# Outputs split by the parity of the position, all FFN-side stores on GpSimd's queue, x loaded for two tiles at once

## The chip, the cores and the metric

The kernel runs on one core of one Trainium2 chip. The metric is the device time of one execution in microseconds, the median over several runs. The engines are named as in the profile: PE (matrix multiply), DVE (vector), ACT (scalar), POOL (GpSimd) and SP (SyncE, which here only issues DMAs). SPq and ACTq are the instruction streams of SP and ACT in which DMA issues stand.

## What is computed

Two blocks follow one another. The first is a long convolution by FFT, per channel, over 4 batches of 12,544 positions with 128 channels; the second is a feed-forward network whose hidden layer is the largest of three products. Cut to what matters:

```
h_filt = (relu(pos_emb @ w1) @ w2) * exp(-0.01 * pos)[:, None]
u = x * v
y = irfft(rfft(u, n=2*S) * rfft(h_filt, n=2*S))[:, :S]      # along the positions
t = (x * y).reshape(B * S, 128)
h = max(t @ W1, t @ W2, t @ W3)                              # 768 hidden columns
out = h @ W_out                                              # 128 columns
```

## The kernel before

Everything is fp32. The 12,544 positions of a batch are 128 residues times 98 (NB). The host lays x and v out by channel, so that the 98 positions of one residue and one channel are one run of 392 bytes; the output is laid out the same way.

**Stages.** First come the filter's spectrum and the convolution of batch 0, with nothing beside them. Then follows the FFN, batch after batch, and beside the FFN of batch b stands the convolution of batch b+1; beside the FFN of batch 3 stands nothing.

**The FFN.** A tile is 4 residues, so 392 columns; a pair is two tiles, and a batch has 16 pairs. `t_load` (L521) brings a tile's part of the convolution's last stage, zt, and its x, xT, both on SP's queue. `t_last` (L538) does the last stage on PE into `yps` and multiplies with xT on DVE (L558, L560) into the tile `gt`, which has 4 buffers. `up` (L565) makes one block of 128 hidden rows: the product `pa`, ACT's Relu of it into `hid` (L570), the product `pb`, DVE's maximum (L573). `products` (L608) multiplies with W_out by a seven-product scheme of Strassen and Winograd's kind, over a 2 x 2 split: the hidden blocks in two halves and the two tiles of the pair; POOL forms its sums s1 to s4 (L589), PE its products into two PSUM banks (`mm`, L619), ACT and DVE the four results c11, c21, c12, c22 (`copied`, L628; `added`, L632). In these names the first index is the tile of the pair and the second the half of the 128 output columns. PE writes each half-tile (two residues) to its own 64 of the 128 partitions. `stored` (L634) writes each result with two DMAs of 49 KB on ACT's queue, so there are eight in a pair.

**The order of the work** is written out by hand. A pair has 12 steps, one for each call of `up`; a list `stream` holds what is due after each step (products 9 steps and more after the pair's start, `LAG`), `SUMS` (L605) the steps of POOL's sums, and `conv_steps` (L475) lays the next batch's convolution over the 192 steps of the batch. Each engine runs its instructions in that order. Within a step `up` comes first, then `stream`, then `t_last`, then the convolution's part. `t_load` is called in steps 0 and 1 of the pair before, `t_last` in steps 5 and 8.

**The convolution beside the FFN** has two phases. In the u phase, for each of 32 (26 for batch 1) units u: `u_load` loads x and v (L337, SP), `u_mul` multiplies (L344, DVE), `u_planes` splits the result into 16-bit planes (L364, L365, POOL), `u_dma` transposes them by DMA (L371, SP), `u_join` puts them together (L380, one half on ACT, one on DVE), `u_first` is the first FFT stage (L140, PE). With s the step of `u_join`, the others stand at s - 13, s - 7, s - 6 and s - 5. In the g phase, for each of 45 groups g: `w_load` and `h_load` (L396, L403, SP), `g_second` on PE, `g_butterfly` on DVE, `g_swap` on ACT, `g_re` and `g_im` on DVE (L430, L433), `g_sum` on POOL (L436), `g_unfold` on DVE (L442, into `ab`), `g_third` on PE (reads `ab` and a second `wt`), `g_pair` on DVE (L468) and `g_store` (L471, a 256 KB DMA on ACT's queue into `zd`). A new group begins about every 2.6 steps.

**Buffers and semaphores.** x and v of the u phase and both `wt` of the g phase share two buffers for each of two tags: the pool `inq` is made twice, and the second, with `bufs=2` (L857), is the one used. The list of instructions shows further that each DMA issued by SP or ACT signals one of eight semaphores (DMAHW0 to 7), taken in turn by both queues together, and that a DMA often waits for the semaphore of the eighth before it; DMAs issued by POOL have eight of their own (DMASW0 to 7).

```
            def stored(n, m, name):                       # L634
                for c in range(2):
                    p0 = 4 * (i + n) + 2 * c
                    nc.scalar.dma_start(dst[64 * m:64 * m + 64, p0:p0 + 2, b, :], ...)
    def t_load(b, i):                                     # L521
        xT = hp.tile([D, 4, NB], FP32, tag="xT", name="xT", bufs=2)
        for c in range(GC):
            nc.sync.dma_start(xT[c * NG:(c + 1) * NG], x[:, 4 * i:4 * i + 4, c, b, :])
```

Of the kernel before, what the change touches and what calls it, by code (L numbers as in the profile page):

```python
# [70 lines left out]
def kernel(  # L71
# [374 lines left out]
    def g_third(b, g):  # L446
        w, ab = ws.pop((g, 1)), abs_.pop(g)
        ps = state["cv"][1].tile([P, 512], FP32, tag="cv", name="ps3")
        for k in range(2):
            for q in range(2):  # L450
                halves_mm(ps[:, (2 * k + q) * D:(2 * k + q + 1) * D], w[:, k, q, :],
                          ab[:, k, q, :], k == 0 and q == 0, True)
        if b == 0:
            zs = state["cv"][0].tile([P, 2, 256], FP32, tag="z", name="zs", bufs=2)
            nc.scalar.copy(zs[:].rearrange("p k f -> p (k f)"), ps[:])
            zss[g] = zs
            g_store(b, g)
        else:
            z1 = state["cv"][0].tile([P, 256], FP32, tag="z1", name="z1", bufs=2)
            nc.scalar.copy(z1[:], ps[:, 256:512])  # L460
            zss[g] = ps, z1

# [58 lines left out]
    def t_load(b, i):  # L521
        zt = hp.tile([N1, 2, 512], FP32, tag="zt", name="zt", bufs=2)
        if b == 0:
            nc.sync.dma_start(
                zt[:], zd[b][:, :, 2 * i:2 * i + 2, :].rearrange("k c t f -> k c (t f)"))
        else:
            for c in range(2):
                nc.sync.dma_start(
                    zt[NK * c:NK * c + NK],
                    zd[b].rearrange("(g a) c t f -> g a c t f", a=2)[  # L530
                        :, :, c, 2 * i:2 * i + 2, :].rearrange("g a t f -> g a (t f)"))
        zts[b, i] = zt
        xT = hp.tile([D, 4, NB], FP32, tag="xT", name="xT", bufs=2)
        for c in range(GC):
            nc.sync.dma_start(xT[c * NG:(c + 1) * NG], x[:, 4 * i:4 * i + 4, c, b, :])
        xTs[b, i] = xT

    def t_last(i):  # L538
        zt = zts.pop(i)
        ps = cps.tile([P, 512], FP32, tag="cv", name="yps")  # L540
        g = hp.tile([D, 4, NB], FP32, tag="g", name="gt", bufs=4)
        y = ps[:, 0:N].rearrange("d (p n) -> d p n", p=4)
        if i[0] == 0:
            for s in range(4):
                for c in range(2):
                    halves_mm(y[:, s, :], zt[:, c, s * D:(s + 1) * D], f4[:, c, :],
                              s == 0 and c == 0, c == 1)
        else:

            h = NB // 2  # L550
            for s in range(4):
                for a in range(2):
                    halves_mm(y[:, s, a * h:a * h + h], zt[:, a, s * D:(s + 1) * D],
                              f4p[:, a, :], s == 0 and a == 0, True)
            y = y.rearrange("d p (a m) -> d p m a", a=2)
        xT = xTs.pop(i)
        if i[0] == 0:
            nc.vector.tensor_tensor(out=g[:], in0=y, in1=xT[:], op=ALU.mult)  # L558
        else:
            nc.vector.tensor_tensor(out=g[:].rearrange("d p (m a) -> d p m a", a=2), in0=y,  # L560
                                    in1=xT[:].rearrange("d p (m a) -> d p m a", a=2),
                                    op=ALU.mult)
        gs[i] = g

    def up(i, f, tag, bufs):  # L565
# [42 lines left out]
    def products(b, i, h, X, Y):  # L608
# [14 lines left out]
        def flat(g):  # L623
            return g[:].rearrange("d p n -> d (p n)")

        def copied(name, ps):
            t[name] = new(name) if name == "p1" else new("o", 3)
            nc.scalar.copy(t[name][:], ps[:, 0:H2])  # L628

        def added(name, a, ps):  # L630
            t[name] = new(name) if name in ("u2", "u3") else new("o", 3)
            nc.vector.tensor_tensor(out=t[name][:], in0=t[a][:], in1=ps[:, 0:H2], op=ALU.add)  # L632
# [9 lines left out]
        plan = (  # L642
            (X, "h11", wo_sb[:, 0:NC, 0:64], True, None, [(copied, "p1", X)], None),
            (Y, "s2", tw[:, 0], True, None, [(added, "u2", "p1", Y)], None),
            (X, "h12", wo_sb[:, NC:, 0:64], False, (m1, first), [(copied, "c11", X)],
             (stored, 0, 0, "c11")),
            (Y, "s3", tw[:, 1], False, (m2, second_), [(added, "u3", "p1", Y)], None),
            (X, "h21", wo_sb[:, 0:NC, 64:128], True, None, [(added, "c22", "u3", X)],
             (stored, 1, 1, "c22")),
            (Y, "h22", tw[:, 2], True, (linx[:], second_), [(added, "c21", "u3", Y)],  # L650
             (stored, 1, 0, "c21")),
            (X, "h12", wo_sb[:, NC:, 64:128], False, (m2, first), [(added, "c12", "u2", X)],
             (stored, 0, 1, "c12")),
        )
        out = []
        for ps, name, w, start, extra, then, store in plan:
            for j in range(NC):
                out.append([lambda ps=ps, name=name, w=w, start=start, j=j: mm(
                    ps, w[:, j, :], h[name, j], start and j == 0)])
            if extra:  # L660
                out.append([lambda ps=ps, extra=extra: mm(ps, extra[0], flat(extra[1]), False)])
            out[-1] += [lambda a=a: a[0](*a[1:]) for a in then]
            out[-1].append(store)
        return out
# [299 lines left out]
```

## Time and profile before

| what | value |
|---|---|
| median of 8 runs | 2498.68 us |
| lowest and highest of them | 2487.79 and 2504.2 us |
| time of the profiled execution | 2504.2 us |
| its span, first to last instruction | 2502.0 us |
| PE busy, share of the span | 2389.0 us, 95% |
| DVE, ACT, POOL busy | 1514.5, 1005.0, 1164.7 us |
| the FFN with a convolution beside it | about 350 to 2050 us of the span |
| the FFN of batch 3, alone | about 2050 to 2490 us |
| DMA issues of the outputs, of x, of zd | 512, 512, 180 |

How to read it: a line of a view of waits names the engine, the tile it was about to write and the line, then what ended its idle time, then the idle microseconds in total, how often, and the longest. A line of a view of windows gives a stretch of the span, its length, then the busy time of PE, PE's weight loads, DVE, ACT and POOL with the number of instructions, then the TensorE clock that was granted (1.00 is full speed), the busy share of the DMA engines and GB/s.

### The profile page before, as it was taken

How to read it: one execution, taken by the hardware profiler on the slowest of the kernel's cores; microseconds unless marked ns; L12 is line 12 of the kernel's file. 1: busy time of each engine (PE TensorE's matmuls, PEld its weight loads, DVE VectorE, ACT ScalarE, POOL GpSimd, SP SyncE). 2: the span in 40 equal slices, each digit the busy share in tenths (PEclk: the TensorE clock that was granted, in tenths of full speed). 3: DMA queues.
4: the chain of work that ended last, by engine and by line, in shares of the span. 5: the costliest groups of instructions: out<-in, count | busy, mean ns of one | idle time of the engine just before them, and what ended most of it. 6: DMA issues, size and time to landing. Idle time of an engine off the chain costs nothing.

```text
span 2502.0 us, 71264 instructions
## 1 busy us (share of the span) xinstructions
PE 2389.0 (95%) x29025; PEld 1689.4 (68%) x29025; DVE 1514.5 (61%) x3044; ACT 1005.0 (40%) x1981; POOL 1164.7 (47%) x1204
## 2 busy tenths in 40 slices
PE   9999999999999999998999998899999999999998
PEld 9888856766666656676766766676666666666665
DVE  5588746576767645566777755547777763333333
ACT  2688824344434323343443423344343432222222
POOL 2022245445545455544554546545455554444444
PEclk9999999999999999999999999999999999999999
DMA  7789779767677458877787747876877753222220
GB/s 169 172 252 278 240 155 175 168 181 206 188 209 208 127 134 170 165 161 193 200 213 201 207 112 165 171 169 170 211 199 200 213 140 91 52 63 61 60 67 20
DMA packets 550736, 408.74 MB, mean 163 GB/s; under 512 B 396388, under 2 KB 442525, under 8 KB 550409
## 3 DMA queue, kind: packets, MB, share of 16 engines
q1 hardware_dynamic: 421760, 315.25, 50.9%
q10 hardware_dynamic: 123273, 74.33, 10.9%
q0 software_dynamic: 5376, 14.62, 2.1%
q8 instruction: 228, 3.74, 0.6%
q14 instruction: 99, 0.81, 0.1%
HBM read 295.76 MB, written 84.67 MB: 152 GB/s over the span
## 4 chain that ended last, share of the span: by engine, by line
PE 81%; DMA 8%; DVE 5%; SPq 2%; issue 2%; ACT 1%; POOL 1%; ACTq 0%; DVEq 0%; POOLq 0%
PE ops L619 18%; PE pb L131 17%; PE pa L131 17%; PE ps L131 13%; PE ps L140 6%; PE yps L131 5%; PE sps L789 3%; DMA turned<-planes 2%; DMA wt<-wt_const 2%; DVE ab L442 2%; DMA zt<-zd 1%; DMA out_dram<-o 1%; DVE zs L468 1%; PE gps L775 1%; PE pm L304 1%
## 5 line engine op out<-in xcount | busy, mean ns | idle before, releaser
L573 DVE TENSOR_TENSOR hid<-hid,pb 128x392 f32<-128x392 f32 x768 | 429.6, 559 | 568.7 <-PE pb L131 481.7
L131 PE MATMUL pb<-gt,w_sb 128*64 128x392 f32 x3072 | 644.8, 496 | 17.7 <-ACT hid L570 17.4
L570 ACT ACTIVATE hid<-pa 128x392 f32<-128x392 f32 x768 | 381.9, 498 | 669.6 <-PE pa L131 575.7
L131 PE MATMUL pa<-gt,w_sb 128*64 128x392 f32 x3072 | 650.2, 500 | 0.0
L131 PEld LDWEIGHTS pb<-gt,w_sb 128*64 128x64 f32 x3072 | 226.2, 138 | 310.3 <-issue 261.5
L589 POOL TENSOR_TENSOR s<-hid 128x392 f32<-128x392 f32 x192 | 215.6, 1123 | 303.5 <-DVE hid L573 275.8
L619 PE MATMUL ops<-hid,wo_sb 128*64 128x196 f32 x3072 | 333.7, 330 | 0.0
L436 POOL TENSOR_TENSOR xt<-xt,xs 128x512 f32<-128x512 f32 x135 | 172.1, 1275 | 322.7 <-DVE xs L433 274.8
L619 PEld LDWEIGHTS ops<-hid,wo_sb 128*64 128x64 f32 x3072 | 226.7, 138 | 135.5 <-issue 116.1
L589 POOL TENSOR_TENSOR s<-hid,s 128x392 f32<-128x392 f32 x192 | 203.0, 1059 | 207.3 <-DVE hid L573 207.2
L589 POOL TENSOR_TENSOR hid<-hid,s 128x392 f32<-128x392 f32 x192 | 211.7, 1108 | 92.1 <-DVE hid L573 68.8
L131 PE MATMUL ps<-ab,wt 128*64 128x128 f32 x2880 | 200.6, 277 | 36.9 <-DVE ab L442 34.9
L131 PE MATMUL ps<-spec,wt 128*64 128x128 f32 x2880 | 200.4, 283 | 27.1 <-DMA wt<-wt_const 23.6
L131 PEld LDWEIGHTS pa<-gt,w_sb 128*64 128x64 f32 x3072 | 206.5, 139 | 18.4 <-issue 2.2
L131 PEld LDWEIGHTS ps<-ab,wt 128*64 128x64 f32 x2880 | 166.5, 137 | 64.6 <-DVE ab L442 52.1
L589 POOL TENSOR_TENSOR hid<-hid 128x392 f32<-128x392 f32 x192 | 205.9, 1092 | 0.0
L442 DVE TENSOR_TENSOR ab<-xt 128x256 f32<-128x256 f32 x360 | 200.9, 599 | 1.6
L131 PEld LDWEIGHTS ps<-spec,wt 128*64 128x64 f32 x2880 | 173.3, 143 | 32.5 <-DVE ab L442 12.5
L140 PE MATMUL ps<-f,uT 98*64 98x90 f32 x4096 | 190.4, 243 | 0.9 <-issue 0.8
L140 PEld LDWEIGHTS ps<-f,uT 98*64 98x64 f32 x4096 | 179.8, 138 | 8.9 <-ACT spec L144 2.5
L430 DVE TENSOR_TENSOR xt<-xt,ht 128x512 f32<-128x512 f32 x180 | 170.8, 949 | 13.7 <-ACT ht L794 13.3
L619 PE MATMUL ops<-s,tw 128*64 128x196 f32 x1536 | 171.6, 329 | 0.0
(103 smaller groups left out, 2800.9 us busy)
## 6 DMA issues: line engine op xcount, KB each, us to landing
wt<-wt_const SPq DMA_DIRECT2D x360, 256.0 KB, 4.1
ht<-hd SPq DMA_DIRECT2D x270, 256.0 KB, 4.5
zd<-zs ACTq DMA_DIRECT2D x180, 256.0 KB, 4.0
zt<-zd SPq DMA_DIRECT2D x192, 180.0 KB, 3.7
ut<-in_xr_dram SPq DMA_DIRECT2D x128, 196.0 KB, 3.2
ut<-in_vr_dram SPq DMA_DIRECT2D x128, 196.0 KB, 3.7
xT<-in_x_dram SPq DMA_DIRECT2D x512, 49.0 KB, 3.0
out_dram<-o ACTq DMA_DIRECT2D x512, 49.0 KB, 3.0
```

The lines of the kernel that those rows point to most:

```text
L131: nc.tensor.matmul(out[64 * h:64 * h + 64], lhsT[:, 64 * h:64 * h + 64], rhs, start=start, stop=stop, skip_group_check=True)
L140: nc.tensor.matmul(ps[64 * c:64 * c + 64, 256 * i + r * N1:256 * i + (r + 1) * N1], a[:, r, :], table[:, c * N1:(c + 1) * N1], start=(i % ...
L304: nc.tensor.matmul(ps[64 * h:64 * h + HH, 512 * r + q * FO:512 * r + (q + 1) * FO], posv[64 * h:64 * h + 64, P - 1 - 2 * (8 * i + q) - r, ...
L430: nc.vector.tensor_tensor(out=xt[:], in0=xt[:], in1=hts[g][:, 0], op=ALU.mult)
L436: eng.tensor_tensor(out=xts[g][:], in0=xts[g][:], in1=xss.pop(g)[:], op=ALU.add)
L442: nc.vector.tensor_tensor(out=ab[:, :, q, :], in0=y[:, :, 0, :], in1=y[:, :, 1, :], op=op)
L468: nc.vector.tensor_tensor(out=zs[:, a], in0=ps[:, 0:256], in1=z1[:], op=op)
L570: nc.scalar.activation(h[:], pa[:, 0:N], Relu)
L573: nc.vector.tensor_tensor(out=h[:], in0=h[:], in1=pb[:, 0:N], op=ALU.max)
L589: nc.gpsimd.tensor_tensor(out=out[:], in0=a[:], in1=b[:], op=op)
L619: nc.tensor.matmul(ps[64 * c:64 * c + 64, 0:H2], w, rhs[:, H2 * c:H2 * c + H2], start=start, stop=True, skip_group_check=True)
L789: nc.tensor.matmul(ps[64 * h:64 * h + 64, (2 * c + k) * 2 * D:(2 * c + k + 1) * 2 * D], G[:, k, c], w2x[:].rearrange("p s d -> p (s d)"), ...
```

## The change

- Each half-tile product now takes residues of one parity: the operand of `mm` is no longer 196 neighbouring columns but two runs of 98. c11 and c21 (the first 64 output columns of both tiles) share one tile `o` of [128, 2, 196], c12 and c22 another; there are two such buffers where there were three of half the size. `stored` writes both results of one column half with two DMAs of 98 KB, so four in a pair, on POOL's queue. The store of m = 0 is due after c21, that of m = 1 after c12.
- `g_store` beside the FFN goes to POOL's queue; in batch 0 it stays on ACT's.
- xT holds 8 residues, loaded in the pair's first `t_load` with four DMAs of 98 KB, where there were eight of 49 KB in two steps.
- `u_load` stands at s - 11 where it stood at s - 13.
- Buffers: z1 from 2 to 1, h12 from 4 to 3, s3 from 4 to 3, the first `inq` pool from 5 to 4.

```diff
-            g_store(b, g)
+            g_store(b, g, nc.scalar)
         else:
-            z1 = state["cv"][0].tile([P, 256], FP32, tag="z1", name="z1", bufs=2)
+            z1 = state["cv"][0].tile([P, 256], FP32, tag="z1", name="z1", bufs=1)
...
-    def g_store(b, g):
-        nc.scalar.dma_start(
+    def g_store(b, g, eng):
+        eng.dma_start(
             zd[b][2 * g:2 * g + 2].rearrange("k c t f -> (c t) k f"), zss.pop(g)[:])
...
-            at(max(0, int(s) - 13), 0, u_load, b, u)
+            at(max(0, int(s) - 11), 0, u_load, b, u)
...
-            at(s + 10, 0, g_store, b, g)
+            at(s + 10, 0, g_store, b, g, nc.gpsimd)
...
-        xT = hp.tile([D, 4, NB], FP32, tag="xT", name="xT", bufs=2)
+        if i % 2:
+            return
+        xT = hp.tile([D, 8, NB], FP32, tag="xT", name="xT", bufs=2)
         for c in range(GC):
-            nc.sync.dma_start(xT[c * NG:(c + 1) * NG], x[:, 4 * i:4 * i + 4, c, b, :])
-        xTs[b, i] = xT
+            nc.sync.dma_start(xT[c * NG:(c + 1) * NG], x[:, 4 * i:4 * i + 8, c, b, :])
+        for n in range(2):
+            xTs[b, i + n] = xT[:, 4 * n:4 * n + 4]
...
-    BUFS = {"h11": 3, "h21": 4, "h22": 4, "h12": 4}
+    BUFS = {"h11": 3, "h21": 4, "h22": 4, "h12": 3}
...
-        h["s3", j] = hp.tile([P, N], FP32, tag="s3", name="s3", bufs=4)
+        h["s3", j] = hp.tile([P, N], FP32, tag="s3", name="s3", bufs=3)
...
-                nc.tensor.matmul(ps[64 * c:64 * c + 64, 0:H2], w,
-                                 rhs[:, H2 * c:H2 * c + H2], start=start, stop=True,
-                                 skip_group_check=True)
+                nc.tensor.matmul(ps[64 * c:64 * c + 64, 0:H2], w, rhs[:, :, c, :],
+                                 start=start, stop=True, skip_group_check=True)
+        def parts(h):
+            return h.rearrange("p (q c n) -> p q c n", q=2, c=2)
+        def place(name):
+            if name[0] != "c":
+                t[name] = new(name)
+                return t[name][:]
+            n, m = int(name[1]) - 1, int(name[2]) - 1
+            if m not in t:
+                t[m] = hp.tile([P, 2, H2], FP32, tag="o", name="o", bufs=2)
+            return t[m][:, n]
...
-        def stored(n, m, name):
+        def stored(m):
             dst = outT.rearrange("d (p b n) -> d p b n", b=B, n=NB)
             for c in range(2):
-                p0 = 4 * (i + n) + 2 * c
-                nc.scalar.dma_start(
-                    dst[64 * m:64 * m + 64, p0:p0 + 2, b, :],
-                    t[name][64 * c:64 * c + 64].rearrange("d (p n) -> d p n", p=2))
+                nc.gpsimd.dma_start(
+                    dst[64 * m:64 * m + 64, 4 * i + c:4 * i + 8:2, b, :],
+                    t[m][64 * c:64 * c + 64].rearrange("d k (q n) -> d (k q) n", q=2))
...
-             (stored, 0, 0, "c11")),
-             (stored, 1, 1, "c22")),
-             (stored, 1, 0, "c21")),
+             (stored, 0)),
-             (stored, 0, 1, "c12")),
+             (stored, 1)),
...
-    inq = ctx.enter_context(tc.tile_pool(name="inq", bufs=5))
+    inq = ctx.enter_context(tc.tile_pool(name="inq", bufs=4))
```

More of the change, by code (lines that the diff above doesn't have):

```diff
@@ L557, in t_last @@
         if i[0] == 0:
-            nc.vector.tensor_tensor(out=g[:], in0=y, in1=xT[:], op=ALU.mult)
+            nc.vector.tensor_tensor(out=g[:], in0=y, in1=xT, op=ALU.mult)
         else:
             nc.vector.tensor_tensor(out=g[:].rearrange("d p (m a) -> d p m a", a=2), in0=y,
-                                    in1=xT[:].rearrange("d p (m a) -> d p m a", a=2),
+                                    in1=xT.rearrange("d p (m a) -> d p m a", a=2),
                                     op=ALU.mult)
@@ L618, in mm @@
             for c in range(2):
-                nc.tensor.matmul(ps[64 * c:64 * c + 64, 0:H2], w,
-                                 rhs[:, H2 * c:H2 * c + H2], start=start, stop=True,
-                                 skip_group_check=True)
-        def flat(g):
-            return g[:].rearrange("d p n -> d (p n)")
+                nc.tensor.matmul(ps[64 * c:64 * c + 64, 0:H2], w, rhs[:, :, c, :],
[10 more added lines that the diff above has]
+            return t[m][:, n]
         def copied(name, ps):
-            t[name] = new(name) if name == "p1" else new("o", 3)
-            nc.scalar.copy(t[name][:], ps[:, 0:H2])
+            nc.scalar.copy(place(name), ps[:, 0:H2])
         def added(name, a, ps):
-            t[name] = new(name) if name in ("u2", "u3") else new("o", 3)
-            nc.vector.tensor_tensor(out=t[name][:], in0=t[a][:], in1=ps[:, 0:H2], op=ALU.add)
-        def stored(n, m, name):
+            nc.vector.tensor_tensor(out=place(name), in0=t[a][:], in1=ps[:, 0:H2], op=ALU.add)
+        def stored(m):
             dst = outT.rearrange("d (p b n) -> d p b n", b=B, n=NB)
             for c in range(2):
-                p0 = 4 * (i + n) + 2 * c
-                nc.scalar.dma_start(
-                    dst[64 * m:64 * m + 64, p0:p0 + 2, b, :],
-                    t[name][64 * c:64 * c + 64].rearrange("d (p n) -> d p n", p=2))
+                nc.gpsimd.dma_start(
+                    dst[64 * m:64 * m + 64, 4 * i + c:4 * i + 8:2, b, :],
+                    t[m][64 * c:64 * c + 64].rearrange("d k (q n) -> d (k q) n", q=2))
         plan = (
@@ L644, in products @@
             (Y, "s2", tw[:, 0], True, None, [(added, "u2", "p1", Y)], None),
-            (X, "h12", wo_sb[:, NC:, 0:64], False, (m1, first), [(copied, "c11", X)],
-             (stored, 0, 0, "c11")),
+            (X, "h12", wo_sb[:, NC:, 0:64], False, (m1, first), [(copied, "c11", X)], None),
             (Y, "s3", tw[:, 1], False, (m2, second_), [(added, "u3", "p1", Y)], None),
-            (X, "h21", wo_sb[:, 0:NC, 64:128], True, None, [(added, "c22", "u3", X)],
-             (stored, 1, 1, "c22")),
+            (X, "h21", wo_sb[:, 0:NC, 64:128], True, None, [(added, "c22", "u3", X)], None),
             (Y, "h22", tw[:, 2], True, (linx[:], second_), [(added, "c21", "u3", Y)],
-             (stored, 1, 0, "c21")),
+             (stored, 0)),
             (X, "h12", wo_sb[:, NC:, 64:128], False, (m2, first), [(added, "c12", "u2", X)],
-             (stored, 0, 1, "c12")),
+             (stored, 1)),
         )
@@ L658, in products @@
                 out.append([lambda ps=ps, name=name, w=w, start=start, j=j: mm(
-                    ps, w[:, j, :], h[name, j], start and j == 0)])
+                    ps, w[:, j, :], parts(h[name, j][:]), start and j == 0)])
             if extra:
-                out.append([lambda ps=ps, extra=extra: mm(ps, extra[0], flat(extra[1]), False)])
+                out.append([lambda ps=ps, extra=extra: mm(ps, extra[0], parts(extra[1][:].rearrange("d p n -> d (p n)")), False)])
             out[-1] += [lambda a=a: a[0](*a[1:]) for a in then]
```

## The prediction

> **What bounds the kernel now.** First the page's busy times, then busy time by stage: the stretch with a convolution beside the FFN (350 to 2050 us) and the FFN alone (2050 to 2490).
>
> ```profile
> span 2502.0 us, 71264 instructions
> PE 2389.0 (95%) x29025; PEld 1689.4 (68%) x29025; DVE 1514.5 (61%) x3044; ACT 1005.0 (40%) x1981; POOL 1164.7 (47%) x1204
> ```
> ```profile
> 350.00:2050.00 1700.00, 1606.27 (x19150) 1130.42 (x19147) 1112.26 (x2214) 665.01 (x1361) 879.54 (x857) 0.98 0.73 181
> 2050.00:2490.00 440.00, 440.00 (x4380) 267.46 (x4378) 159.85 (x327) 113.01 (x240) 206.24 (x207) 1.00 0.24 60
> ```
>
> Alone, the FFN is bound by PE: 440 of 440 us at clock 1.00. Nothing done to queues can gain there. Beside a convolution PE idles 1700 - 1606.27 = 93.7 us. Before 350 us the change edits nothing but a tile's shape. So the case is decided by those 93.7 us and what they cost in clock. PE's waits in that stretch:
>
> ```profile
> PE ps L131 <- DVE ab L442: 34.3, 37, 2.5
> PE ps L131 <- DMA wt<-wt_const: 23.6, 14, 4.5
> PE pb L131 <- ACT hid L570: 16.2, 13, 3.8
> PE yps L131 <- DMA zt<-zd: 13.3, 6, 4.6
> ```
>
> Two of the four are loads that came late, and the third is one in disguise: ACT's `hid` stands in its queue behind `uT` (L380), and the page of waits has ACT waiting 116.9 us in 40 waits for the transposed `turned`. Why do loads come late, when DMA engines are busy 0.73 of that stretch? SP's own waits there:
>
> ```profile
> SPq L396 <- PE ps L131: 319.0, 92, 10.2
> SPq L337 <- POOL planes L365: 110.3, 59, 4.3
> SPq L403 <- DMA out_dram<-o: 53.2, 25, 4.7
> ...
> SPq L396 <- DMA zd<-zs: 39.6, 10, 6.1
> SPq L535 <- DMA out_dram<-o: 37.2, 20, 4.0
> ...
> SPq L535 <- DMA zd<-zs: 20.6, 10, 3.2
> ```
>
> The first two are true waits for a buffer. The others are odd: a load of ht, wt or x needs nothing from a store of outputs. They wait because DMAs of SP and ACT share eight semaphores, and the eighth before has not landed. The four lines sum to 150.6 us of a queue that works in order, so a wt behind them is late. The clock makes PE's idle time dearer:
>
> ```profile
> 1214.00:1218.00 4.00, 1.61 (x18) 0.88 (x16) 4.00 (x9) 1.74 (x3) 2.47 (x2) 1.00 1.00 238
> 1218.00:1222.00 4.00, 4.00 (x34) 3.00 (x34) 0.84 (x2) 0.83 (x3) 1.33 (x1) 0.57 0.52 145
> ```
>
> After 2.39 idle us in the first four, the next four ran at clock 0.57. Over 350 to 2050, in stretches of 50 us, the clock is 0.97 in fifteen, 0.96 in one and 0.93 in two, 1.00 in the rest: 0.63 x 50 = 32 us of PE lost.
>
> **The change, part by part.**
>
> *SP and the shared semaphores.* Over the 48 pairs with a convolution beside them, a pair had 8 stores of outputs, 8 loads of x, 4 of zt, and 5.6 of wt, 5.6 of ht, 2.8 of zd (270, 270, 135 over 48): 34 DMAs on the eight semaphores. Now 4 of x, 4 of zt, 11.2: 19. The x issues (median 0.430 us) fall by 256; an issue of ut with four times the runs of the old x takes 0.38 to 0.51, so a larger x should not issue slower: 110 us of SP gained; at least nothing, if the time goes with bytes. The wt waits stand where zt and x loads come together. I take 80% of 23.6: **-18.9**.
>
> *u_load two steps later.* Its two buffers come free only with `planes` of the unit before last, which the 110.3 us above show. Every transpose queued behind such a blocked load waits too. Laying out `conv_steps` by hand: before, the last load ahead of a transpose waits for a `planes` step so late that 2.9 to 3.1 steps are left to the join; after, 4.5. A step is 440/192 = 2.3 us, so 6.7 to 7.1 us become 10.3, against 1.27 us of issue and 3.8 to land for a transpose, often two in a row. The load itself loses nothing, being held by its buffer anyway; if that cover is gone, it costs 2 steps, 4.6 us of lead against 3.7 to land, and the DVE multiply (already waiting 40.1 us in 31 waits) would be late. I take 3/4 of 16.2, **-12.2**, and two thirds of the zt waits, which sit behind the same loads: 13.3 x 2/3 = **-8.9**.
>
> *ab stays.* DVE stands before `gt`, whose buffer PE still reads (75.3 us in 26 waits for L560, 44.5 in 13 for L558, on `ops`), and is 72% busy (71.75 of 100 us at 1950). Nothing here changes that: 0 of 34.3.
>
> *Clock.* Idle time falls by 40.0 of 93.7; in proportion, 32 x 0.43 = **-14**.
>
> The Trainium skill (TensorE: Matmul & The Clock Gate, Why this matters for your kernels) allows idle gaps up to about 3 us without a drop. The drop at 1218 followed 2.39 us, so the rows decide; by the page only the longest waits would pay, an estimate of some 10 us in place of 14.
>
> *ACT* loses 512 issues of 0.619 us and 135 of 0.377 (368 us). It is 39% busy in the stretch and mostly waits for PE: 0 by itself. Below nothing is possible (its queue too stopped for the semaphores); that is kept for the large-gain rival.
>
> *POOL* gains 256 + 135 issues. The trace has no such store there; the nearest rows are hd (64 partitions, 2 KB runs: 0.528 us) and the w_out load (384 runs: 0.780). Ours have 256 runs; by runs, 0.528 + 0.252 x 192/320 = 0.68. In a stretch pair (1700/48 = 35 us) that is 6.8 x 0.68 = 4.6 us on a POOL busy 18.3. Upper end: the longest issue of this store, on ACT, 1.73. What queues behind: the listing shows the zd store right ahead of the next group's `xt` sum, which releases ab. The store waits for `zs`, the sum for the multiply after it on DVE (L433, 0.743), so the issue lies beside that multiply: 0.68 - 0.74 is below nothing. Allowing 0.1 at each of the 37 ab waits: **+3.7**. Output stores wait for DVE's c21 and c12 in steps where POOL's sums wait for DVE as well (312.9 us): 0.
>
> The Trainium skill (SBUF — State Buffer, SBUF: two separate sides) speaks against the move: descriptors of a GpSimd DMA can't be written while DVE holds the shared port, and it gives about 3.1 us for one that takes 0.62 alone. The 90 hd issues took 0.527 to 0.556 while DVE was busy 44 of each 50 us, so this trace doesn't show it; at 3.1 us (an estimate) POOL would need 18.3 + 21 of 35 us and the change would lose over 150 us.
>
> *Buffers.* h12 and s3: the old reader on PE is one to two steps earlier than the new writer, 0. z1: `g_pair` stands a step or two before the next `third`, 0, at worst a few tenths at some of ACT's 114 waits. The first `inq` pool holds no tile: 0. The two o buffers: stored at steps 19 and 21, rewritten at 25 and 28; 4 steps are 9 us against 4.4 to land: 0.
>
> *Operand of two runs.* No row has it. A weight load that jumps at every column (L304, 41 columns) takes 163 ns against 138 for 64 neighbouring ones: 25 ns for 40 jumps, so one jump in each of 6400 products is 0 to 4 us. I take 0, as one jump is nearer to none than to 40.
>
> *The end.* The last stores: 2 x 0.68 for 2 x 0.62, and 4.4 to land (hd) for 3.0: **+1.4**.
>
> Sum: -18.9 - 12.2 - 8.9 - 14 + 3.7 + 1.4 = **-49**. The profiled execution took 2504.2 us (span 2502.0, 2.2 around it), so 2455; it lies 5.5 above the median of 2498.68, and against that the forecast is **2450**.
>
> **The rivals.**
>
> *Small gain.* SP's largest waits are for buffers, 319.0 and 110.3, and those stay: then wt is late as before, and only half of the hid and zt waits go: -14.8, clock -5, +5 of costs and half of the wt, -6: -21, **2478**. For it: two buffers for wt. Against it: the wt waits fall where x and zt are loaded, not at every group.
>
> *Large gain.* ACT, no longer stopped, and an earlier x (28.7 us of DVE waits on xT) also free DVE: all of 59.4 us and a third of ab with 75% of the clock: 53.1 + 11.4 + 24 - 5 = -83, **2415**.
>
> *Stalls come back.* With loads in time, DVE (72% busy) is late next, and ab grows by what wt gave up: **2499**. For it: ab is already the largest of the four.
>
> *Slower.* The store ahead of each `xt` sum becomes the releaser of ab: at 1.73 us an issue it is 0.99 later in each of 135 groups, +133 - 53, **2579**. It decides from (49 + 4)/135 = 0.39 us over 0.74, so an issue of 1.13 us. Against it: 0.78 is the longest row on POOL.
>
> **How the numbers follow.** Forecast (2430 to 2470) 0.50, small gain 0.18, large gain 0.12, stalls come back 0.07, slower 0.13. The likeliest is 2450. The range 2395 to 2505 holds all but the slower case and the tails: about 0.83; it takes in 0 to 4 us for the operand, an issue of 0.53 to about 1.15 us, and no gain. A measurement of this kernel tells about 0.3% (7.5 us) from no change: faster 0.80, same 0.07, slower 0.13.
>
> **What would show it.** SP's waits on out_dram and zd gone, but for the first zt of a batch; PE's wt wait under 6 us, hid under 6, zt under 6, ab about 34; POOL's new issues 0.6 to 0.8 us; the clock 0.99 over the stretch; the FFN alone again at 27.5 us a pair, or the operand costs. The prediction is wrong if ab's wait grows past 50, if POOL's issues exceed 1.1 us, or if the lone FFN's pairs lengthen.

## The result, and the profile after

The changed kernel takes **2491.79 us** (median of 24 runs, 2484.75 to 2498.68), the kernel before, run beside it, 2500.82 us (median of 66). The ratio is **0.9964 [0.9954, 0.9973]**: faster by 9 us, where 49 were forecast. First the page's head, with the busy times of the engines.

```profile
span 2489.4 us, 70518 instructions
...
PE 2374.7 (95%) x29025; PEld 1654.7 (66%) x29025; DVE 1623.5 (65%) x3044; ACT 1008.6 (41%) x1981; POOL 1389.7 (56%) x1595
```

PE does the same 29025 matmuls in 14.3 us less (2389.0 before): that is the clock, granted at 0.990 in the mean of this execution and at 0.984 before. (The profiled execution of before, 2504.2 us, lies 3.4 above its median, so part of the 14.3 is that execution's.) Its idle time, span less busy, is 114.7 us where it was 113.0. So the whole gain came from the clock, and none from the waits, though waits were what the change was forecast to remove. DVE, which got no work, is busy 109 us longer. POOL has 225 us more: its new stores add 97.0 + 162.0 = 259, and its other work, its sums above all, takes 34 less. By stage, in the columns of the prediction:

```profile
350.00:2040.00 1690.00, 1593.73 (x19160) 1094.24 (x19158) 1221.43 (x2215) 670.13 (x1365) 1060.09 (x1175) 0.99 0.76 182
2040.00:2480.00 440.00, 440.00 (x4382) 269.77 (x4380) 160.36 (x326) 112.56 (x239) 250.13 (x278) 1.00 0.24 60
```

The lone FFN is as it was: 440 of 440 us, 4382 matmuls where there were 4380. The operand of two runs costs nothing that shows. Beside the convolution PE idles 1690 - 1593.73 = 96.3 us (93.7 before). Whose waits these are, between 350 and 2050 us:

```profile
PE ps L131 <- DVE ab L442: 82.8, 65, 4.6
PE ps L131 <- issue: 3.8, 4, 1.7
PE pb L131 <- ACT hid L573: 3.0, 6, 0.6
...
PE ps L131 <- DMA wt<-wt_const: 0.2, 1, 0.2
```

The late loads are gone (wt 23.6 to 0.2, hid 16.2 to 3.0, zt 13.3 to none), 49.9 us in all. The wait for `ab`, of which the prediction said "0 of 34.3", grew by 48.5. SP's waits in the same stretch:

```profile
SPq L396 <- PE ps L131: 641.6, 128, 12.8
SPq L337 <- POOL planes L365: 103.3, 47, 11.2
SPq L528 <- DMA zd<-zs: 58.6, 5, 19.5
```

The 150.6 us for landings of out_dram and zd are gone but for the first `zt` of a batch, which truly needs its zd. SP now stands for free `wt` buffers, which is where a queue that is early should stand.

What DVE does with its extra time is in the groups of its instructions (instructions, busy us, mean ns, idle time ahead). Before, then after:

```profile
L442 DVE TENSOR_TENSOR ab<-xt 128x256 f32<-128x256 f32 x360 | 200.9, 599 | 1.6
...
L468 DVE TENSOR_TENSOR zs<-ps,z 128x256 f32<-128x256 f32 x270 | 101.1, 416 | 0.0
```
```profile
L442 DVE TENSOR_TENSOR ab<-xt 128x256 f32<-128x256 f32 x360 | 253.3, 743 | 1.6
...
L468 DVE TENSOR_TENSOR zs<-ps,z 128x256 f32<-128x256 f32 x270 | 101.0, 416 | 0.0
```

The same 360 instructions on the same shapes take 52.4 us more. L430 goes from 949 to 1124 ns, and L380, a copy of 16-bit values within SBUF, from 780 to 975. L468, as large as L442 but with one operand in PSUM, stays at 416 ns. One instruction of L442 lasted at most 1.35 us before, and 4.86 now. That one stands on the chain of work that ended last (start, us, what):

```profile
1101.74 0.15 DVE hid L576
1101.89 0.24 issue
1102.13 4.86 DVE ab L442
1106.99 0.04 issue
1107.03 1.89 PE ps L131 x16
```

POOL's timeline over the same microseconds (start, us, line, operation, tiles):

```profile
1100.30 1.25 POOL L647 DMA_DIRECT2D out_dram<-o  x2 [1.59 <-DVE o L642]
1101.56 1.03 POOL L592 TENSOR_TENSOR s<-hid,s 128x392 f32<-128x392 f32 x1
1102.54 1.27 POOL L436 TENSOR_TENSOR xt<-xt,xs 128x512 f32<-128x512 f32 x1
1103.76 2.93 POOL L592 TENSOR_TENSOR hid<-hid 128x392 f32<-128x392 f32 x3
```

POOL stood 1.59 us at the head of two stores, issued them for 1.25, and then ran five sums without a break, to 1106.69. DVE's `ab`, started in the first of them, ended 0.30 us after the last. PE, which needed it, idled 4.55 us, and its clock fell (same columns as by stage):

```profile
1104.00:1108.00 4.00, 0.97 (x10) 0.83 (x12) 4.00 (x4) 0.00 (x0) 2.69 (x3) 0.91 0.00 0
1108.00:1112.00 4.00, 4.00 (x28) 2.27 (x26) 1.75 (x5) 2.00 (x4) 0.00 (x0) 0.66 0.43 136
```

How often POOL stands at a store is in its waits between 350 and 2050 us:

```profile
POOL s L592 <- DVE hid L576: 135.5, 91, 5.6
POOL zd L472 <- DVE zs L468: 127.4, 61, 7.1
POOL out_dram L647 <- DVE o L642: 108.7, 49, 7.1
POOL xt L436 <- DVE xs L433: 80.5, 69, 5.4
```

Before, the first line was 312.9 and the last 274.8, and no store stood among POOL's waits. Part of POOL's idle time has moved: it stands 236.1 us at stores that wait for DVE, with sums behind them in its queue. (Another 42.7 us at output stores, in 13 waits, have no releaser in the profile, so 236 is the lower figure.) When a store is let go, the sums behind it come in a row, as in the timeline.

The trace allows a count of this. Every DVE instruction between 450 and 2050 us is put down by what POOL ran during it (mean ns, number, longest):

```
                             before              after
L442, POOL does nothing      417 (136)           414 (59)
L442, POOL issues a DMA      -                   415 (93)
L442, POOL runs sums         904 (132; 1353)     1641 (64; 4861)
L430, POOL does nothing      682 (24)            681 (20)
L430, POOL issues a DMA      -                   681 (24)
L430, POOL runs sums         1111 (111; 1589)    1571 (66; 3712)
L468, POOL runs sums         416 (159; 421)      416 (152; 420)
```

(Instructions that met both an issue and a sum are left out: L442 1142 ns, 54 of them.) A store's issue costs DVE nothing. Beside sums, an instruction with two operands in SBUF takes about half a microsecond more than alone in before, and 0.9 (L430) to 1.2 us (L442) more in after, where sums come in rows.

Two more counts from the trace tie this to PE. During PE's waits for `ab` an L442 was already standing, past the 0.415 us that it takes alone, for 37.0 of the 82.8 us in after, and for 4.2 of 34.3 before. So 32.8 of the 48.5 us that came are L442's own standing; that the rest is `ab` begun late on a DVE busy 109 us longer is argued, not counted. And in each of the 135 groups beside the FFN, the `xt` sum had ended at least 2.79 us before its L442 began (3.02 before the change): `ab` never waited for its sum.

### The profile page after: what moved, and what is told of

It reads as the page before. It is cut to its first block, busy times and chain, and to the rows that moved or that the text cites. A ratio compares the mean times of both kernels' runs of the same rounds, so it can differ in the third digit from the quotient of the medians.

```text
span 2489.4 us, 70518 instructions
## 1 busy us (share of the span) xinstructions
PE 2374.7 (95%) x29025; PEld 1654.7 (66%) x29025; DVE 1623.5 (65%) x3044; ACT 1008.6 (41%) x1981; POOL 1389.7 (56%) x1595
## 4 chain that ended last, share of the span: by engine, by line
PE 81%; DVE 11%; DMA 3%; issue 3%; POOL 1%; ACT 1%; SPq 0%; ACTq 0%; DVEq 0%; POOLq 0%
PE pb L131 17%; PE pa L131 17%; PE ops L622 17%; PE ps L131 12%; PE ps L140 7%; PE yps L131 4%; DVE ab L442 4%; PE sps L796 3%; DVE hid L576 2%; DVE zs L468 1%; PE pm L304 1%; DMA wt<-wt_const 1%; PE gps L782 1%; DVE xt L430 1%; DVE xs L433 1%
## 5 line engine op out<-in xcount | busy, mean ns | idle before, releaser
L131 PE MATMUL pa<-gt,w_sb 128*64 128x392 f32 x3072 | 642.1, 496 | 0.1
L622 PE MATMUL ops<-hid,wo_sb 128*64 128x196 f32 x3072 | 331.5, 329 | 0.4 <-DVE hid L576 0.4
L647 POOL DMA_DIRECT2D out_dram<-o x256 | 162.0, 637 | 276.0 <-DVE o L642 109.6
L622 PEld LDWEIGHTS ops<-hid,wo_sb 128*64 128x64 f32 x3072 | 221.3, 137 | 139.6 <-issue 114.3
L131 PE MATMUL ps<-ab,wt 128*64 128x128 f32 x2880 | 204.6, 280 | 86.4 <-DVE ab L442 83.4
L592 POOL TENSOR_TENSOR s<-hid 128x392 f32<-128x392 f32 x192 | 205.9, 1073 | 135.0 <-DVE hid L576 108.9
L442 DVE TENSOR_TENSOR ab<-xt 128x256 f32<-128x256 f32 x360 | 253.3, 743 | 1.6
L592 POOL TENSOR_TENSOR hid<-hid,s 128x392 f32<-128x392 f32 x192 | 205.9, 1078 | 43.4 <-DVE hid L576 24.6
L131 PEld LDWEIGHTS pa<-gt,w_sb 128*64 128x64 f32 x3072 | 200.8, 138 | 20.5 <-issue 1.7
L430 DVE TENSOR_TENSOR xt<-xt,ht 128x512 f32<-128x512 f32 x180 | 202.4, 1124 | 14.0 <-ACT ht L801 13.6
L131 PE MATMUL ps<-spec,wt 128*64 128x128 f32 x2880 | 190.6, 275 | 2.9 <-issue 2.0
L140 PEld LDWEIGHTS ps<-f,uT 98*64 98x64 f32 x4096 | 176.7, 137 | 13.2 <-ACT spec L144 4.0
L622 PE MATMUL ops<-s,tw 128*64 128x196 f32 x1536 | 170.7, 328 | 0.0
```

The source lines that it names most:

```text
L131: nc.tensor.matmul(out[64 * h:64 * h + 64], lhsT[:, 64 * h:64 * h + 64], rhs, start=start, stop=stop, skip_group_check=True)
L140: nc.tensor.matmul(ps[64 * c:64 * c + 64, 256 * i + r * N1:256 * i + (r + 1) * N1], a[:, r, :], table[:, c * N1:(c + 1) * N1], start=(i % ...
L430: nc.vector.tensor_tensor(out=xt[:], in0=xt[:], in1=hts[g][:, 0], op=ALU.mult)
L442: nc.vector.tensor_tensor(out=ab[:, :, q, :], in0=y[:, :, 0, :], in1=y[:, :, 1, :], op=op)
L622: nc.tensor.matmul(ps[64 * c:64 * c + 64, 0:H2], w, rhs[:, :, c, :], start=start, stop=True, skip_group_check=True)
L647: nc.gpsimd.dma_start(dst[64 * m:64 * m + 64, 4 * i + c:4 * i + 8:2, b, :], t[m][64 * c:64 * c + 64].rearrange("d k (q n) -> d (k q) n", q=2))
```

## The experiments

Three theories stood against each other. **A**: the stores hold POOL up and add to its work, its sums then come in rows, and DVE's instructions with two operands in SBUF stand beside them; so `ab` is late. **B**: the zd store alone does it, by standing right ahead of the `xt` sum that `ab` is made from. **C**: whatever POOL does, DVE is late next once loads come in time.

Times are medians, each with its ratio to the kernel before on the same chip; the chips differ (there the kernel before took 2510 to 2518 us), so both columns are given: a ratio compares a run with the kernel before on its own chip, but the changed kernel was not run on those chips. PE busy and idle are of the profiled execution's span; the waits for `ab` and `wt` are PE's between 350 and 2050 us (a dash where none is listed).

| kernel | median us | ratio | PE busy | PE idle | ab | wt |
|---|---|---|---|---|---|---|
| before | 2500.82 | 1 | 2389.0 | 113.0 | 34.3 | 23.6 |
| after | 2491.79 | 0.9964 [0.9954, 0.9973] | 2374.7 | 114.7 | 82.8 | 0.2 |
| e1, zd by ACT | 2456.72 | 0.9767 [0.9724, 0.981] | 2366.1 | 89.1 | 49.3 | 5.2 |
| e2, outputs by ACT | 2472.44 | 0.9838 [0.9794, 0.9881] | 2377.7 | 100.2 | 71.1 | - |
| e3, both by ACT | 2432.93 | 0.9672 [0.9623, 0.9721] | 2363.1 | 69.3 | 34.6 | 3.4 |
| e4, before + u_load late | 2477.05 | 0.985 [0.9803, 0.9897] | 2374.2 | 94.6 | 34.4 | 22.7 |
| e5, stores two steps later | 2469.41 | 0.9813 [0.9773, 0.9853] | 2370.1 | 92.5 | 57.8 | 4.0 |
| e6, after, memsets for sums | 2403.78 | one run | 2348.8 | 53.2 | 26.7 | - |
| e7, zd by POOL behind the sum | 2438.58 | 0.9727 [0.9691, 0.9763] | 2366.5 | 71.3 | 43.1 | 1.4 |
| e8, e4 + merged x | 2458.01 | 0.9805 [0.9762, 0.9848] | 2373.5 | 86.4 | 34.3 | 22.9 |
| e9, e3 + gt of five | 2394.56 | 0.9556 [0.952, 0.9593] | 2345.4 | 43.8 | 8.5 | 8.4 |
| e10, e3, memsets for sums | 2408.57 | one run | 2349.3 | 57.5 | 24.5 | 5.4 |
| e11, after + gt of five | 2437.85 | 0.9703 [0.9685, 0.9722] | 2362.0 | 76.2 | 43.8 | 0.9 |
| e12, e7 + gt of five | 2389.57 | 0.9512 [0.9493, 0.9532] | 2348.6 | 38.2 | 14.7 | 2.0 |

**e1: the zd store back on ACT's queue**, all else as after.

```diff
-            at(s + 10, 0, g_store, b, g, nc.gpsimd)
+            at(s + 10, 0, g_store, b, g, nc.scalar)
```

> The changed kernel, with the stores of zd back on ACT's queue and the output stores still on POOL's. The changed kernel's profile has PE waiting 82.8 us for ab (before: 34.3) and DVE busy 1623.5 us (before: 1514.5). Theory A, the sums run in a row: POOL, held at a store until DVE has made its data, runs its sums without a gap afterwards, and DVE's instructions with two operands in SBUF (ab, L430) stand until the row ends. The zd stores are 127 of the 236 us for which POOL stood before a store, so about half goes: DVE busy near 1570, ab wait near 55, time near 2470. Theory B, the order of POOL's queue: only the zd store stands directly ahead of the xt sum that ab reads, so all goes: ab wait near 35, time near 2450. Theory C, the stalls come back: DVE is the next limit whatever POOL does; ab wait stays near 80, time near 2490.

Measured 2456.72 us; `ab` falls from 82.8 to 49.3, between the 55 of A and the 35 of B. That is most of the extra wait but not all of it, and DVE is still busy 1583.3 us, its longest `ab` 4.87 us.

**e2: the output stores back on ACT's queue**, zd on POOL's.

```diff
-                nc.gpsimd.dma_start(
+                nc.scalar.dma_start(
```

> The changed kernel, with the output stores (four for a pair, by parity) back on ACT's queue and the zd stores still on POOL's. Theory A (sums run in a row after a held store): the other half goes, DVE busy near 1570, ab wait near 55, time near 2470. Theory B (the zd store ahead of the xt sum): nothing goes, ab wait near 80, time near 2490. Theory C (DVE is next anyway): ab wait near 80, time near 2490.

Measured 2472.44 us; `ab` 71.1. POOL stands 155.5 us at zd stores, and DVE is busy 1563.2 us, as A expected; but `ab` lies between its 55 and the 80 of B and C (the profile is of the slowest of the four executions, 2479.67 us). The outputs are the smaller part.

**e3: both back on ACT's queue**, by the two edits above.

> The changed kernel with all stores on ACT's queue: four output stores by parity, x for two tiles at once, u_load two steps later, smaller buffers. ACT's DMAs take the shared semaphores again, 26 DMAs of SP and ACT a pair where there were 34 before and 19 in the changed kernel. Theories A and B: ab wait near 35, DVE busy near 1515, wt wait of PE between 0 and 10 us, hid and zt waits under 6, time near 2455. Theory C: ab wait near 80 and DVE busy near 1515, time near 2490.

Measured 2432.93 us. PE's waits, 350 to 2050 us:

```profile
PE ps L131 <- DVE ab L442: 34.6, 37, 2.5
PE ps L131 <- issue: 3.8, 4, 1.7
PE ps L131 <- DMA wt<-wt_const: 3.4, 5, 1.3
```

The loads are in time and `ab` is back at 34.6 with it: C falls. The time lies 22 us under the forecast of A and B; PE is busy 2363.1 us, 11.6 less than in after, which is clock again. By stores on POOL, outputs add 49.3 - 34.6 = 14.7 us, zd adds 71.1 - 34.6 = 36.5; both together add 48.2, nearly the sum of 51.2. DVE is busy 1518.4 us, as before the change.

**e4: the kernel before with `u_load` two steps later**, nothing else.

```diff
-            at(max(0, int(s) - 13), 0, u_load, b, u)
+            at(max(0, int(s) - 11), 0, u_load, b, u)
```

> The kernel before with one edit: u_load two steps later. The prediction's step on u_load alone: hid wait from 16.2 to about 4 and zt wait from 13.3 to about 4, wt 23.6 and ab 34.3 as they were, so 21 us of idle time and about 7 of clock less: near 2471. Theory C (what is freed comes back elsewhere): within 8 us of the kernel before, with ab or wt grown by 20.

Measured 2477.05 us: this line alone gives 1.5%, more than the whole change. The waits for zt are gone and those for ACT's `hid` fall from 16.2 to 3.6 us, though 6.6 us for DVE's `hid` come in; SP's wait for `planes` (L337) falls from 110.3 to 42.5; wt stays at 22.7.

**e5: both stores two steps later**, still on POOL, so that what they wait for is done.

```diff
-            at(s + 10, 0, g_store, b, g, nc.gpsimd)
+            at(min(s + 12, 185), 0, g_store, b, g, nc.gpsimd)
...
-                            later(at_ + 1, *fn)
+                            later(at_ + 3, *fn)
```

> The changed kernel with POOL's stores due two steps later (zd at step s + 12, the last ones no later than step 185; outputs three steps after their result in place of one). The same number of DMA issues, 0.64 and 0.72 us each, but POOL should not stand before them. Theory A (held stores make the sums run in a row): the 236 us for which POOL stood before stores fall under 60, DVE busy falls to about 1540, ab wait to about 40, time near 2455. If it is POOL's added work of 260 us and not the standing, DVE busy stays above 1600 and the time near 2490. Theory B (the zd store directly ahead of the xt sum): it now stands after it, ab wait near 35. Theory C: ab near 80, 2490.

Measured 2469.41 us. POOL stands 0.5 us at zd stores and 1.7 at the outputs, where it stood 236 us, and `ab` falls to 57.8: 25.0 of the 48.2 us go with the standing, 23.2 stay; the run lies between A's forecast (DVE busy 1540, `ab` 40) and the one for added work (1600), with DVE busy 1571.5 us. What stays fits A's second half: POOL has 391 issues more than in e3 and is busy 1402.4 us, for 1156.7. Beside sums alone L442 takes 897 ns here, as in before, but 1621 beside a sum and an issue together (24 of them, the longest 3.39 us).

**e6: after, with each of the FFN's sums replaced by two memsets** of the same tile, so that POOL works nearly as long (2 x 0.43 us for 1.07) but reads nothing. The sums are left out of the computation.

```diff
-        nc.gpsimd.tensor_tensor(out=out[:], in0=a[:], in1=b[:], op=op)
+        for _ in range(2):
+            nc.gpsimd.memset(out[:], 0.0)
```

> The changed kernel with each of POOL's sums in the FFN (s1 to s4) left out, and two memsets of the same tile in its place: POOL is busy for nearly as long and still held at its stores, but reads no SBUF there. Theory A (DVE's instructions with two operands in SBUF stand for POOL's sums): ab (L442) near 0.42 us and L430 near 0.70 us each beside these memsets, but for those beside the xt sums; DVE busy under 1500, ab wait under 30. Theory B: ab wait stays near 80, since the zd store is still ahead of the xt sum. Theory C: DVE freed of some 150 us, so ab falls with it as in theory A; it is told apart by the other runs.

One run, 2403.78 us. First POOL's waits, then the group of `ab`:

```profile
POOL zd L472 <- DVE zs L468: 219.9, 89, 7.9
...
POOL out_dram L648 <- DVE o L643: 97.6, 35, 7.2
```
```profile
L442 DVE TENSOR_TENSOR ab<-xt 128x256 f32<-128x256 f32 x360 | 154.5, 471 | 1.6
```

The stores stand ahead of the sums as in after, at zd for longer, yet `ab`'s wait is 26.7 us. B falls as a cause by itself, as it does by the 2.79 us or more that lie between sum and L442. Beside a memset alone L442 takes 418 ns (86 of them) and L430 685 (43): it is not POOL's being busy that DVE stands for, but sums that read SBUF. The run also makes DVE 202 us less busy than in after (1421.6), so a smaller cost of another kind could hide in its slack.

**e7: outputs by ACT (e2), and the zd store on POOL two steps later**, behind the next `xt` sum, by e5's first edit.

> Output stores on ACT's queue, zd stores on POOL's, but due two steps later (s + 12, no later than step 185), so that each stands behind the xt sum that it stood ahead of. Compare with the kernel that has only the zd stores on POOL (ab wait 71.1, DVE busy 1563.2, median 2472) and the one with all stores on ACT (34.6, 1518.4, 2433). If the delay of the xt sum is what the zd store costs: ab wait near 38, time near 2437. If it is that POOL's sums are pushed together and DVE stands for them, the same number of issues still stands in the row: ab wait near 55, DVE busy above 1545, time near 2455.

Measured 2438.58 us; `ab` 43.1, DVE busy 1542.7 us: nearer the forecast for the delayed sum (38) than the other (55). Of the zd store's 36.5 us, 28.0 go with the edit and 8.5 stay. But the edit takes away two things at once, the place right ahead of an `xt` sum (105 of the 135 stores in e2, 35 here) and POOL's standing, which is 0.5 us at zd stores where it was 155.5 in e2. The delay of the sum is not what it saves: in e2 too each `xt` sum had ended at least 2.79 us before its L442. What falls is L442's own standing during PE's waits for `ab`, from 33.8 us in e2 to 5.8. Which of place and standing brings the sums beside L442, e7 does not tell.

**e8: e4 with x loaded for two tiles at once** (the change's xT, and h12 and s3 with 3 buffers each to make room).

> The kernel before with u_load two steps later (alone: ratio 0.985, wt wait 22.7) and x loaded for two tiles at once, h12 and s3 with three buffers for room; outputs and stores as before: 30 DMAs of SP and ACT a pair in place of 34. If fewer x issues are what brings wt in time: wt wait under 8, time near 2445. If it is the stores that held the shared semaphores (26 a pair with four output stores): wt wait 15 to 20, time near 2465.

Measured 2458.01 us against e4's 2477.05 on another chip, ratios 0.9805 and 0.985 with intervals that overlap; wt stays at 22.9. Merging x does not by itself bring wt in time. What is left between e8 and e3 (wt 3.4) is the outputs' part: four stores in a pair where there were eight. This is by elimination; no run merges the outputs without x. SP's wait for out_dram at L396 and L403 is 68.6 and 49.7 us in e8 and 0 and 1.5 in e3, where the stores are on the shared semaphores all the same. SP stands there for landings of zd instead, 71.1 and 50.6 us in e3 (28.9 and 34.0 in e8). So the semaphores still stop SP, for 123.2 us at these two lines where it was 110.3 before the change, and yet wt costs PE only 3.4. Why the stops for outputs made wt late and those for zd hardly do stays open.

**e9: e3 with a fifth buffer for `gt`**, whose wait the prediction named as DVE's largest; a buffer of xs pays for it.

```diff
-        g = hp.tile([D, 4, NB], FP32, tag="g", name="gt", bufs=4)
+        g = hp.tile([D, 4, NB], FP32, tag="g", name="gt", bufs=5)
...
-    state = {"turn": cps, "cv": (cvp, cps), "xb": 4, "xsb": 4}
+    state = {"turn": cps, "cv": (cvp, cps), "xb": 4, "xsb": 3}
```

> All stores on ACT's queue (ab wait 34.6, median 2433), with five buffers for gt in place of four, and three in place of four for the xs and turned tiles, for room. The prediction held that ab is late because DVE stands before gt until PE has read the old one (75.3 and 44.5 us in the stretch before). If so: that wait under 30 us, ab wait under 15, time near 2400. If DVE's own load makes ab late: ab wait stays above 28, time near 2430.

Measured 2394.56 us. DVE no longer waits for `ops` at `gt` (91.3 us in 31 waits in e3 for L563, 38.1 for L561), and `ab` falls to 8.5. Most of the 34 us that were there from the start stood behind `gt`.

**e10: e3 with e6's memsets**, the sums left out of the computation again; it closes the square of stores and sums.

> All stores on ACT's queue, and POOL's sums in the FFN left out, with two memsets of the same tile in place of each. Beside the same with stores on POOL's queue (2403.8 us, ab wait 26.7, DVE busy 1421.6) it gives what the stores cost when POOL's sums don't read SBUF. If they cost only through the sums that DVE stands for: ab wait 20 to 27, time within 8 us of 2403.8. If they cost by delaying the xt sum as well: ab wait under 10, time near 2385.

One run, 2408.57 us; `ab` 24.5. The square, in us of PE's wait for `ab`:

| | stores on ACT | stores on POOL | difference |
|---|---|---|---|
| POOL's sums read SBUF | 34.6 (e3) | 82.8 (after) | 48.2 |
| memsets in their place | 24.5 (e10) | 26.7 (e6) | 2.2 |

With sums that read SBUF the stores cost 48.2 us, without them 2.2, each cell of the lower row from one run. Within the slack named at e6, the stores cost PE through the sums that DVE stands for. That is A.

**e11: after with e9's two edits.**

> The changed kernel, all stores on POOL's queue, with five buffers for gt and three for the xs and turned tiles. With all stores on ACT's queue the same edit took the ab wait from 34.6 to 8.5 us and the ratio from 0.967 to 0.956. If what POOL's stores cost (48 us of ab wait) is separate from DVE's standing before gt: ab wait near 55, time near 2440. If both add to the same backlog of DVE, it falls by more than the 26 us: ab wait near 25, time near 2410.

Measured 2437.85 us; `ab` 43.8. The fifth buffer helps here too, but DVE is busy 1636.8 us and 35.3 us more of the wait is left than in e9: room does not undo the rows of sums.

**e12: e7 with e9's two edits.**

> Five buffers for gt, output stores on ACT's queue, zd stores on POOL's behind the xt sum. Beside all stores on ACT (2394.6, wt wait 8.4, ab wait 8.5): the shared semaphores are freer by 2.8 DMAs a pair, so wt wait near 3; if zd on POOL still pushes the sums together (ab 43.1 for 34.6 without the fifth buffer), ab wait near 15. Sum: within 8 us of 2394.

Measured 2389.57 us, ratio 0.9512 [0.9493, 0.9532], faster than before and after. PE's waits:

```profile
PE ps L131 <- DVE ab L442: 14.7, 29, 0.7
PE ps L131 <- issue: 2.0, 3, 0.7
PE ps L131 <- DMA wt<-wt_const: 2.0, 2, 1.1
```

Against e9 it has 6.2 us more of `ab` and 6.4 less of wt. The intervals of the two ratios overlap, so which queue should carry zd, once it is behind the sum, is not told by these runs.

## Why the prediction was right in sign and wrong in size

*What bounds the kernel* held: the lone FFN stayed at 440 of 440, and everything happened in PE's idle time and clock beside the convolution. The sign owes much to luck: the idle time, which was to fall by 40, rose by 1.7, and what is left is the clock. The prediction named its own sign of being wrong, `ab`'s wait past 50 us, and that is what came (82.8).

*SP and the shared semaphores*: forecast -18.9, measured -23.4. Right in size, but the mechanism is not as it was put. POOL's queue was not needed (e3), the larger x was not enough (e8), and by elimination it is the halved output stores that count. SP's waiting as such does not decide: it stands 123.2 us at its wt and ht loads for landings in e3, no less than before, with wt at 3.4.

*u_load*: forecast -12.2 and -8.9, measured -13.2 and -13.3. Right, and e4 shows that this one line does it, but for some waits on DVE's `hid`.

*Clock*: forecast -14, measured -14.3 of PE's busy time, but not for the reason given. The forecast took it in proportion to idle time, which did not fall. Counted from the trace over 350 to 2050 us, PE had ten gaps of 2 us or more before, 34.7 us in all, and four after, 14.5 us; gaps of 1 to 2 us went from 37.4 to 59.2. Between these two traces the loss goes with the long gaps, but the other runs do not bear that out as a rule: e2 has twelve such gaps, 32.8 us, and PE is busy 11.3 us less than before, while e1 (11.3 us of them) and e7 (2.5) have the same PE busy. The drop to 0.57 that the prediction shows followed two waits of 1.68 and 0.71 us. Over all fourteen traces PE's busy time goes with total idle time at least as closely as with the long gaps (correlation 0.94 and 0.87): where idle time did fall (e3, 69.3 us), the clock gave 25.9. So the forecast's proportion is not refuted in general; why the clock gave 14.3 here at the same idle time stays open, and that the number fits is luck.

*POOL and ab stays*: **this is the step that failed.** "Allowing 0.1 at each of the 37 ab waits: +3.7" and "Nothing here changes that: 0 of 34.3" together became +48.5. That DVE stands before `gt` was right (e9), though the 72% is of one stretch of 100 us; over 350 to 2050 DVE was busy 65%. The price of an issue was right: 0.68 forecast, 0.64 measured for the outputs and 0.72 for zd, none near 1.1. Wrong was what it was used for. The prediction asked how much later the store makes the sum behind it, and found cover in DVE's multiply; a later sum indeed costs nothing, since it ends 2.79 us or more before it is read. It did not ask how long the store stands at POOL's head (236 us), nor what the sums do to DVE when they come. The trace of before held the sign of it: L442 at 599 ns in the mean, 417 beside an idle POOL and 904 beside a sum, was there to be counted. *Output stores: 0* failed with it: their steps were ones "where POOL's sums wait for DVE as well", but a store that stands there holds back the sums behind it, and they cost 14.7 us (e3 against e1).

*Buffers and the operand* cost nothing that shows: `pb` waits 3.0 us for `hid`, and the operand is at 0 of its 0 to 4. (The row taken for it was a weight load; the runs of 98 are in the operand that streams past the weights.) *The end*: from PE's last matmul to the end of the span there are 7.5 us before and 5.7 after, so +1.4 was -1.8: ACT issued eight stores there, POOL four.

The sum over the terms: -49.9 of late loads, +48.5 of `ab`, some 3 us of small waits (idle time +1.7 in all), -14.3 of clock: -12.6 us of span, and -9.0 between the medians.

*The rivals*: "stalls come back" gave the number that came nearest, 2499, for a reason that e3 refutes: with the same early loads and the stores off POOL, `ab` stays at 34.6. "Slower" looked at the right queue, but at the delay of the `xt` sum, which costs nothing, and so asked for a price of 1.13 us an issue that was not needed. "Large gain" names 59.4 us of waits and sums 53.1 of them; with 59.4 it would be 6 us lower, which decides nothing.

The Trainium skill (SBUF — State Buffer, SBUF: two separate sides) says that a vector instruction with two inputs in SBUF and a GpSimd operation that reads SBUF exclude each other, the one that starts first holding the port for its whole instruction. The runs agree: 904 and 1641 ns beside sums, 414 beside nothing, 418 beside memsets, 416 with one operand in PSUM. By that rule alone, an estimate, an instruction would stand for one sum, 1.28 us in the mean for the longer kind, and take some 1.7; the one at 1102.13 stood until all five were through. The prediction cited this section for the issue of the stores, whose figure of 3.1 us no run shows (0.62 to 0.76), and passed over the sentence beside it, which was the one that mattered.

## What to carry to other kernels

Before a DMA issue is moved to GpSimd, do not ask what the issue costs, but what the store waits for and which sums stand behind it: here the stores on POOL took back nearly all that the change had won from its queues (48.5 of 49.9 us), about half by standing 236 us and half with no standing left (e5). Where GpSimd's operations and VectorE's read SBUF side by side, look up in the trace of before what VectorE's two-operand instructions take beside them and alone; what packed GpSimd's work closer here, made that difference larger (487 to 1227 ns for L442). Take one edit at a time: a single line (e4) was worth 1.5%, a buffer that the trace had named and the change did not touch (the fifth `gt`, e3 to e9) 1.2% by the ratios and 1.6% by the medians, and the stores' move to POOL cost 2.4% by the medians and 2.9% by the ratios (after against e3, on different chips), which the sum of all the edits hid.

## What the runs showed of the hardware that was not expected

- A DVE instruction of 0.41 us stood through five consecutive POOL sums, 4.86 us: it was not let in between them. In the same trace, PE's clock was 0.66 in the 4 us after its wait of 4.55.
- POOL's issue of a DMA beside DVE's work cost neither: L442 415 ns and L430 681 beside an issue, the issues 0.638 (98 KB in 256 runs) and 0.717 us (256 KB in 256 runs), the latter 0.712 to 0.737 at all times.
- POOL's memsets cost DVE nothing (418 and 685 ns), and its sums were not slowed by the crowding (1.07 us in the mean; 1.10 before). Only DVE paid.
- One jump in the operand that streams past the weights, 98 columns after 98, cost a matmul nothing: 328 ns in the mean at L622 in the lone FFN, 329 before (L619).
- SP's stops for landings of other DMAs, at its wt and ht loads, do not by their sum tell how late wt is: 110.3 us of them went with a wt wait of 23.6 before, 123.2 with 3.4 in e3.
